# Window attention with global tokens: the order of a head's products on TensorE, and transposes of short key chunks

## The chip, the cores and the metric

The kernel runs on one core of one Trainium2 chip. The metric is the device time of one execution in microseconds, the median of the timed runs. Engine names in the rows: PE is TensorE's matrix product and PEld its weight load, DVE is VectorE, ACT is ScalarE, POOL is GpSimd, SP is the queue that issues most DMAs.

## The reference

There are 8 batches of 8 heads, 512 local tokens, 32 global tokens and a head width of 64. Global queries attend to all keys; local queries attend to the global keys and to a window of 32 positions on either side. The result goes through a feed-forward layer (width 512 to 2048 and back) with a squared ReLU, a scale and a bias.

```python
s_g = scale * q_g @ concat(k_g, k_l).T
out_g = sm(s_g) @ concat(v_g, v_l)
s_ll = where(abs(i - j) <= 32, scale * q_l @ k_l.T, -1e9)
a_l = sm(concat(scale * q_l @ k_g.T, s_ll))
out_l = a_l @ concat(v_g, v_l)
x = concat(out_g, out_l).transpose(0, 2, 1, 3).reshape(B * S, H * D)
h = x @ w_in
out = (s * relu(h) ** 2 + b) @ w_out
```

## The kernel before

A "half" is 256 local queries of one batch. There are 16 halves, and in each the 8 heads are worked one after the other; j counts them, 128 turns in all. The first 16 turns are worked as pairs of heads in plain float32; from turn 16 each head is worked alone, and its operands are split into a high and a low part so that the fast float32 format of TensorE can be used. A head's 256 queries are two blocks of 128; each block sees a strip of 192 or 224 keys, 416 in both blocks together (`COLS`). In the transposed probabilities each block has two chunks of keys: a whole one, 128 keys seen by all 128 queries, and a short one, of which only 64 or 96 keys and as many query columns are used (`CHUNKS`, whose entries are first key column, first query, number of queries).

Four kinds of products belong to a head on TensorE. The scores (line 363) are four: two blocks, each with the high and the low part of the queries as weights and the block's keys as moving columns (192 or 224). The global queries' product (line 376) has 64 weight columns and 256 or 288 moving ones. The transposes (line 316) are four, one for each chunk: the chunk of the probabilities is the weights and an identity matrix is what moves. The product with the values (line 407) is four, one for each chunk, with the values as 128 weight columns and 128, 192 or 256 moving ones.

The loop over j is a pipeline. In turn j TensorE computes the scores of head j, the transposes of head j-1 and the value products of head j-2, and then two pieces of the feed-forward, which lags by 10 turns: 24 products with 256 moving columns for piece m = j-10 (`ffn_in`, line 528) and 12 products with 512 for piece m-1 (`ffn_out`, line 561). Every eight turns there are also the transposes (line 455) and value products (line 478) of the global queries' rows. In PSUM there is one bank for the scores, one for the transposes (tag "t"), one for the value products and one for the global queries' products (tag "g"); the banks "t" and "g" are shared with the global rows' own transposes.

The order of TensorE's instructions is written out from turn 25 on (`ORDERED`, `manual_schedule`): from there the program's order is TensorE's order. Before turn 25, and on the other engines all along, a scheduler with a cost model places the instructions. Turn 25 itself issues its global queries' product late, behind the feed-forward piece.

In a turn of a first half the order on TensorE is: one score product, the global queries' product, three score products, two value products, three transposes, two value products, one transpose. In a second half the global queries' product stands behind the third score product. Before the transposes, `p_transposes` takes the two short chunks first. A transpose of a short chunk that begins at query 0 moves 96 columns of the identity, the others 128; all of them load 128 key columns as weights. Where a chunk needs fewer than 128 keys, the packed values have rows of zeros at the unused keys, and what stands there in the probabilities is multiplied by zero.

After a head's transposes, ScalarE (line 396) and VectorE (line 397) read the transposed probabilities out of PSUM and split them. After the global queries' product ScalarE (line 384) copies its low part and VectorE (line 385) adds the two.

Of the kernel before, what the change touches and what calls it, by code (L numbers as in the profile page):

```python
# [10 lines left out]
F32 = mybir.dt.float32  # L11
# [10 lines left out]
P = 128  # L22
# [10 lines left out]
CHUNKS = {  # L33
# [11 lines left out]
NF = 16  # L45
AHEAD = 0
LAG = 10
ORDERED = 25
# [19 lines left out]
def window_attention_then_ffn(ctx: ExitStack, tc: tile.TileContext, qd, qp, qg, kw, vw, vg, w_in, w_out, sv, bv, out):  # L68
# [23 lines left out]

    keep_busy(WARM_FIRST, "warm0")


# [200 lines left out]
    def chunks(j):  # L296
        b, hf, h = slot(j)
        o = 0
        for blk in range(2):
            for c in range(2):  # L300
                c0, q0, n = CHUNKS[hf, blk][c]
                yield blk, c, c0, q0, n, slice(o, o + n)
                o += n

# [3 lines left out]
    def p_transposes(j):  # L308
        sm = st_.pop(("p", j))
        p_t = ps.tile([P, 512], F32, tag="t", name=f"ps_t{j}")  # L310
        first = 64 if slot(j)[1] == 0 else 0
        st_["pst", j] = p_t[:, first:first + NC]
        for blk, c, c0, q0, n, o in sorted(chunks(j), key=lambda x: x[1]):
            at = first + o.start - q0
            q = 96 if c == 0 and q0 == 0 else P
            nc.tensor.transpose(out=p_t[:, at:at + q], in_=sm[0:q, c0:c0 + P], identity=ident[0:q, 0:q])  # L316
            yield
# [35 lines left out]
    def scores(j):  # L353
        b, hf, h = slot(j)
        ks, qs = st_.pop(("ks", j)), st_.pop(("qs", j))
        p_s = ps.tile([P, 512], F32, tag="s", name=f"ps_s{j}")
        late = j == ORDERED
        if not late:
            p_g = ps.tile([P, 512], F32, tag="g", name=f"ps_g{j}")
        for blk in range(2):  # L360
            cols = COLS[hf, blk]
            for a in range(2):
                nc.tensor.matmul(  # L363
                    p_s[:, cols], lhsT=qs[:, a, blk * P:(blk + 1) * P], rhs=ks[:, cols], start=(a == 0), stop=(a == 1),
                )
                if blk == hf and a == 0 and not late:
                    g_product(j, ks, p_g)
        softmax([j], [p_s])
        if late:
            st_["late", j] = ks  # L370
        else:
            g_sum(j, p_g)

# [12 lines left out]

    def late_scores(j):
        if ("late", j) in st_:
            p_g = ps.tile([P, 512], F32, tag="g", name=f"ps_g{j}")
            g_product(j, st_.pop(("late", j)), p_g)  # L390
            g_sum(j, p_g)
# [32 lines left out]

    def transposes_and_pv(jt, jp):
        t = p_transposes(jt) if NF <= jt < NS else iter(())
        p = pv_products(jp) if NF <= jp < NS else iter(())
        for which in (p, p, t, t, t, p, p, t):
            next(which, None)
        list(p), list(t)  # L430
        if NF <= jp < NS:
            pv_sum(jp)
        if NF <= jt < NS:
            p_split(jt)


# [11 lines left out]
    def g_transposes(b, g):  # L448
        sg = st_["sg", b, g]
        pg = st_["pg", b, g] = sb.tile([P, 5, 4, 2, SG], F32R, tag="pg", name=f"pg{b}_{g}", bufs=1)  # L450
        for c0, c1, tag in ((0, 4, "g"), (4, 5, "t")) if b else ((4, 5, "g"), (0, 4, "t")):
            p_t = ps.tile([P, 4, P], F32, tag=tag, name=f"ps_tg{b}_{g}_{c0}")
            for c in range(c0, c1):
                s0 = min(c * P, SGW - P)
                nc.tensor.transpose(out=p_t[:, c - c0, :], in_=sg[:, s0:s0 + P], identity=ident)
            v = p_t[:, 0:c1 - c0].rearrange("p c (h q) -> p (c h) q", h=4)
            ph, pl = (pg[:, c0:c1, :, i, :].rearrange("p c h q -> p (c h) q") for i in range(2))
            with tc.high_priority():
                nc.scalar.copy(out=ph, in_=v)
                nc.vector.tensor_sub(out=pl, in0=v, in1=f32(ph))  # L460
            yield
# [41 lines left out]
    def xg_split(t):  # L503
        xs = sb.tile([P, 8 * HALF + 56], F32R, tag="xs", name=f"xs{t}", bufs=1)
        xs = xs[:, 0:8 * HALF].rearrange("p (i c q) -> p i c q", i=2, c=4)
        for i in range(2):
            xr = sb.tile([P, 2 * NC], F32, tag="pt", name=f"xgr{i}")[:, 0:DM]
            nc.sync.dma_start(xr, xg_d[i * P:(i + 1) * P, :])
            p_t = ps.tile([P, 4, P], F32, tag="ts"[i], name=f"ps_xg{i}")
            for c in range(4):  # L510
                nc.tensor.transpose(out=p_t[:, c, :], in_=xr[:, c * P:(c + 1) * P], identity=ident)
            q = slice(i * P, (i + 1) * P)
            nc.scalar.copy(out=xs[:, 0, :, q], in_=p_t)
            nc.vector.tensor_sub(out=xs[:, 1, :, q], in0=p_t, in1=f32(xs[:, 0, :, q]))
        xs_[t] = xs
# [98 lines left out]
    for j in range(NM + LAG + 2):  # L614
# [18 lines left out]
        tr(j - 1)  # L633
        transposes_and_pv(j - 1, j - 2)
        vsp(j - 1)
# [7 lines left out]
        if 0 <= m < NM:  # L643
            ffn_in(m)
            late_scores(j)
            if m % 8 == 7:
# [88 lines left out]
```

## Time and profile before

| what | value |
|---|---|
| median of three runs | 1035.42 us (1033.2 to 1035.54) |
| the profiled execution, first to last instruction | 1034.0 us |
| its own time beside this span | the profile gives the span alone |
| TensorE products busy | 996.6 us, 96% of the span |
| TensorE weight loads busy | 903.5 us, 87% |
| VectorE, ScalarE, GpSimd busy | 805.9, 706.1, 300.9 us |
| mean granted TensorE clock | 0.982 of full speed |
| feed-forward products, lines 528 and 561, busy | 422.7 and 404.1 us |
| transposes, line 316, busy | 95.9 us in 512 in the page's group |
| value products, line 407; scores, line 363 | 90.7 and 77.5 us |

The two feed-forward groups make up 65% of the chain that ended last, the transposes 4%, the value products 4%, the scores 4%. Products overlap one another in the profile, since the next one starts while the last one drains: the duration of a single product is longer than the time by which it moves the end, and a sum of durations is not a time. The difference between the ends of two successive products is. Some records of products can be missing from a trace.

### The profile page before, as it was taken

How to read it: one execution, taken by the hardware profiler on the slowest of the kernel's cores; microseconds unless marked ns; L12 is line 12 of the kernel's file. 1: busy time of each engine (PE TensorE's matmuls, PEld its weight loads, DVE VectorE, ACT ScalarE, POOL GpSimd, SP SyncE). 2: the span in 40 equal slices, each digit the busy share in tenths (PEclk: the TensorE clock that was granted, in tenths of full speed). 3: DMA queues.
4: the chain of work that ended last, by engine and by line, in shares of the span. 5: the costliest groups of instructions: out<-in, count | busy, mean ns of one | idle time of the engine just before them, and what ended most of it. 6: DMA issues, size and time to landing. Idle time of an engine off the chain costs nothing.

```text
span 1034.0 us, 20232 instructions
## 1 busy us (share of the span) xinstructions
PE 996.6 (96%) x7060; PEld 903.5 (87%) x7060; DVE 805.9 (78%) x2036; ACT 706.1 (68%) x1786; POOL 300.9 (29%) x365
## 2 busy tenths in 40 slices
PE   5689999999999999999999999999999999999996
PEld 2368898899999999999999999999999999999995
DVE  6999778888878888888888888888888888873321
ACT  5986777677676777777677777777677777653221
POOL 0000444233433333333333432343323443211000
PEclk8869999999999999999999999999999999999999
DMA  8952222212321222213221222222221321101000
GB/s 326 344 177 68 88 81 84 76 59 86 91 70 57 71 88 76 74 55 97 78 79 53 70 90 71 79 63 91 73 78 58 95 72 45 42 24 35 12 21 21
DMA packets 62254, 85.73 MB, mean 83 GB/s; under 512 B 7368, under 2 KB 49352, under 8 KB 62152
## 3 DMA queue, kind: packets, MB, share of 16 engines
q1 hardware_dynamic: 61864, 83.39, 25.4%
q8 instruction: 56, 0.92, 0.4%
q10 hardware_dynamic: 288, 1.05, 0.3%
q14 instruction: 46, 0.38, 0.1%
HBM read 74.97 MB, written 9.44 MB: 82 GB/s over the span
## 4 chain that ended last, share of the span: by engine, by line
PE 80%; DVE 9%; ACT 4%; DMA 3%; issue 2%; POOL 0%; SPq 0%; ACTq 0%; DVEq 0%; POOLq 0%
PE ps_h L528 33%; PE acc L561 32%; PE ps_t L316 4%; PE ps_o L407 4%; PE ps_s L363 4%; DVE g L543 1%; PE ps_og L478 1%; PE ps_g L376 1%; DMA rq<-in_qd 1%; DVE x L420 1%; DVE r L535 1%; DVE sm L236 1%; DMA wst<-in_w_in 1%; ACT sm L227 1%; ACT kq L197 1%
## 5 line engine op out<-in xcount | busy, mean ns | idle before, releaser
L528 PE MATMUL ps_h<-xs,w 128*128 128x256 f32 x3264 | 422.7, 284 | 3.4 <-ACT xs L499 2.7
L528 PEld LDWEIGHTS ps_h<-xs,w 128*128 128x128 f32 x3264 | 399.8, 190 | 7.4 <-ACT xs L499 3.1
L561 PE MATMUL acc<-w,g 128*128 128x512 f32 x1632 | 404.1, 395 | 0.0
L561 PEld LDWEIGHTS acc<-w,g 128*128 128x128 f32 x1632 | 294.6, 188 | 57.6 <-ACT r L534 0.5
L543 DVE SCALAR_TENSOR_TENSOR g<-r,b_t,g 128x512 fp32r<-128x512 f32 x136 | 118.3, 870 | 56.1 <-ACT g L542 55.7
L534 ACT ACTIVATE r<-ps_h 128x512 f32<-128x512 f32 x136 | 81.2, 597 | 112.0 <-PE ps_h L528 105.7
L542 ACT ACTIVATE g<-r,b_t 128x512 fp32r<-128x512 f32 x136 | 98.4, 724 | 78.4 <-DVE r L535 77.7
L535 DVE SCALAR_TENSOR_TENSOR r<-ps_h,s_t,r 128x512 f32<-128x512 f32 x136 | 101.4, 746 | 64.3 <-ACT r L534 64.3
L200 POOL TENSOR_TENSOR kq<-rq,kq 128x256 fp32r<-128x256 f32 x112 | 85.2, 761 | 191.8 <-ACT kq L199 187.4
L198 POOL TENSOR_TENSOR kq<-rk,kq 64x416 fp32r<-64x416 f32 x56 | 61.3, 1095 | 257.7 <-ACT kq L197 249.5
L227 ACT ACTIVATE sm<-sm,nm 128x224 f32<-128x224 f32 (+1 forms) x256 | 119.7, 469 | 5.0 <-DVE nm L221 4.6
L208 POOL TENSOR_TENSOR vs<-rv,vs 128x256 fp32r<-128x256 f32 x112 | 91.6, 818 | 95.4 <-ACT vs L207 90.1
L316 PE MATMUL ps_t<-ident,sm 128*128 128x128 f32 (+1 forms) x512 | 95.9, 274 | 12.6 <-ACT ptp L323 8.2
L384 ACT COPY tg<-ps_g 32x256 f32<-32x256 f32 (+1 forms) x112 | 42.3, 378 | 72.1 <-PE ps_g L376 71.5
L407 PE MATMUL ps_o<-pt,vs 128*128 128x256 f32 x448 | 90.7, 284 | 0.0
L418 DVE TENSOR_TENSOR u<-ps_o,u 128x256 f32<-128x256 f32 x112 | 47.4, 423 | 45.0 <-ACT u L417 43.2
L221 DVE CUSTOM_DVE_ANT_0 sm<-ps_s,mask 128x192 f32<-128x192 f32 (+1 forms) x224 | 74.7, 371 | 9.7 <-PE ps_s L363 9.5
L470 POOL TENSOR_TENSOR vsg<-rvg,vsg 128x320 fp32r<-128x320 f32 x64 | 56.7, 906 | 79.3 <-ACT vsg L469 79.3
L363 PEld LDWEIGHTS ps_s<-kq 128*128 128x128 f32 x448 | 71.6, 189 | 7.1
L363 PE MATMUL ps_s<-kq 128*128 128x192 f32 (+1 forms) x448 | 77.5, 265 | 0.0
L316 PEld LDWEIGHTS ps_t<-ident,sm 128*128 128x128 f32 (+1 forms) x512 | 57.7, 143 | 17.3 <-ACT ptp L323 9.8
L407 PEld LDWEIGHTS ps_o<-pt,vs 128*128 128x128 f32 x448 | 67.8, 190 | 0.3
(76 smaller groups left out, 1211.3 us busy)
## 6 DMA issues: line engine op xcount, KB each, us to landing
rq<-in_qd SPq DMA_DIRECT2D x112, 128.0 KB, 2.3
rv<-in_vw SPq DMA_DIRECT2D x112, 128.0 KB, 2.0
rk<-in_kw SPq DMA_DIRECT2D x56, 208.0 KB, 2.4
rvg<-in_vg SPq DMA_DIRECT2D x32, 320.0 KB, 2.9
out<-o SPq DMA_DIRECT2D x34, 256.0 KB, 2.0
wst<-in_w_in SPq DMA_DIRECT2D x15, 512.0 KB, 6.1
wst<-in_w_out SPq DMA_DIRECT2D x15, 512.0 KB, 6.7
rvp<-in_vw SPq DMA_DIRECT2D x8, 256.0 KB, 4.7
```

The lines of the kernel that those rows point to most:

```text
L200: nc.gpsimd.tensor_sub(out=qs[:, 1, :], in0=rq, in1=f32(qs[:, 0, :]))
L208: nc.gpsimd.tensor_sub(out=vs[:, :, 1, :], in0=rv4, in1=f32(vs[:, :, 0, :]))
L227: nc.scalar.activation(out=p, in_=p, func=AF.Exp, bias=nm[:, n:n + 1], scale=-1.0, accum_out=ss[:, n:n + 1],)
L316: nc.tensor.transpose(out=p_t[:, at:at + q], in_=sm[0:q, c0:c0 + P], identity=ident[0:q, 0:q])
L363: nc.tensor.matmul(p_s[:, cols], lhsT=qs[:, a, blk * P:(blk + 1) * P], rhs=ks[:, cols], start=(a == 0), stop=(a == 1),)
L407: nc.tensor.matmul(p_o[:, blk, :, q0:q0 + n], lhsT=vs[:, 2 * blk + c], rhs=pt[:, :, o], start=(c == 1), stop=(c == 0),)
L528: nc.tensor.matmul(p_h[:, k], lhsT=wi[f][:, a, c, :], rhs=xs[:, e, c, :], start=(n == 0), stop=(n == 11),)
L534: nc.scalar.activation(out=r, in_=p_h, func=AF.Relu)
L535: nc.vector.scalar_tensor_tensor(out=r, in0=p_h, scalar=s_t, in1=r, op0=ALU.mult, op1=ALU.mult)
L542: nc.scalar.activation(out=g[:, 0], in_=r, func=AF.Identity, bias=b_t)
L543: nc.vector.scalar_tensor_tensor(out=g[:, 1], in0=r, scalar=b_t, in1=f32(g[:, 0]), op0=ALU.add, op1=ALU.subtract,)
L561: nc.tensor.matmul(oacc[t][i], lhsT=g[:, a, k, i * P:(i + 1) * P], rhs=wo[f][:, e, :], start=(pr == 0 and n == 0), stop=(pr == 7 and n == 5),)
```

## The change

The short chunks are transposed with only as many key columns as they use: 64 or 96 weight columns instead of 128, so that only 64 or 96 partitions of PSUM are written. The rest of the partitions must hold finite numbers, and so the bank of the transposes becomes one buffer for the whole kernel, `t_bank`, which VectorE sets to zero once. In the first half's first block the short chunk's 64 keys are now read from column 128, at the first partitions, and the packed values have their zero rows behind them instead of ahead. The short chunk of the second half's second block, 64 keys wide, now moves 128 identity columns where it moved 96; it stands last in the transposed columns, so that nothing overlaps it.

The order within a head changes: the whole chunk of the first block is transposed first, then the short chunks (96 keys, then 64), and the other whole chunk last. On TensorE a turn is now: four score products, three transposes, the global queries' product, two value products, one transpose, two value products. The readers of the global queries' product are issued at its new place too. Turn 25 still issues it late.

```diff
-    (0, 0): ((64, 64, 64), (0, 0, 128)),
+    (0, 0): ((128, 64, 64), (0, 0, 128)),
...
     keep_busy(WARM_FIRST, "warm0")
+    t_bank = ps.tile([P, 512], F32, tag="t", name="t_bank")
+    nc.vector.memset(t_bank, 0.0)
...
     def chunks(j):
         b, hf, h = slot(j)
         o = 0
-        for blk in range(2):
-            for c in range(2):
-                c0, q0, n = CHUNKS[hf, blk][c]
-                yield blk, c, c0, q0, n, slice(o, o + n)
-                o += n
+        for blk, c in ((0, 0), (0, 1), (1, hf), (1, 1 - hf)):
+            c0, q0, n = CHUNKS[hf, blk][c]
+            yield blk, c, c0, q0, n, slice(o, o + n)
+            o += n
...
     def p_transposes(j):
         sm = st_.pop(("p", j))
-        p_t = ps.tile([P, 512], F32, tag="t", name=f"ps_t{j}")
+        p_t = t_bank
         first = 64 if slot(j)[1] == 0 else 0
         st_["pst", j] = p_t[:, first:first + NC]
-        for blk, c, c0, q0, n, o in sorted(chunks(j), key=lambda x: x[1]):
+        whole, short = [], []
+        for chunk in chunks(j):
+            (whole if chunk[1] else short).append(chunk)
+        short.sort(key=lambda x: -x[4])
+        for blk, c, c0, q0, n, o in (whole[0], *short, whole[1]):
             at = first + o.start - q0
-            q = 96 if c == 0 and q0 == 0 else P
-            nc.tensor.transpose(out=p_t[:, at:at + q], in_=sm[0:q, c0:c0 + P], identity=ident[0:q, 0:q])
+            q = 96 if n == 96 else P
+            keys = P if c else n
+            nc.tensor.transpose(out=p_t[0:keys, at:at + q], in_=sm[0:q, c0:c0 + keys], identity=ident[0:q, 0:q])
             yield
...
     def scores(j):
...
-        late = j == ORDERED
-        if not late:
-            p_g = ps.tile([P, 512], F32, tag="g", name=f"ps_g{j}")
...
-                if blk == hf and a == 0 and not late:
-                    g_product(j, ks, p_g)
         softmax([j], [p_s])
-        if late:
-            st_["late", j] = ks
-        else:
-            g_sum(j, p_g)
+        st_["gk", j] = ks
...
-    def late_scores(j):
-        if ("late", j) in st_:
+    def g_scores(j):
+        if NF <= j < NS:
             p_g = ps.tile([P, 512], F32, tag="g", name=f"ps_g{j}")
-            g_product(j, st_.pop(("late", j)), p_g)
+            g_product(j, st_.pop(("gk", j)), p_g)
             g_sum(j, p_g)
...
-    def transposes_and_pv(jt, jp):
+    def transposes_and_pv(j, jt, jp):
         t = p_transposes(jt) if NF <= jt < NS else iter(())
         p = pv_products(jp) if NF <= jp < NS else iter(())
-        for which in (p, p, t, t, t, p, p, t):
-            next(which, None)
-        list(p), list(t)
+        for _ in range(3):
+            next(t, None)
+        g_late = j == ORDERED
+        if not g_late:
+            g_scores(j)
+        next(p, None), next(p, None)
+        list(t)
+        list(p)
         if NF <= jp < NS:
             pv_sum(jp)
         if NF <= jt < NS:
             p_split(jt)
+        return g_late
...
-            p_t = ps.tile([P, 4, P], F32, tag=tag, name=f"ps_tg{b}_{g}_{c0}")
+            if tag == "t":
+                p_t = t_bank.rearrange("p (c q) -> p c q", c=4)
+            else:
+                p_t = ps.tile([P, 4, P], F32, tag=tag, name=f"ps_tg{b}_{g}_{c0}")
...
-        transposes_and_pv(j - 1, j - 2)
+        g_late = transposes_and_pv(j, j - 1, j - 2)
...
             ffn_in(m)
-            late_scores(j)
+            if g_late:
+                g_scores(j)
...
-        _np.concatenate([z[:, :, 0:64], w[0][:, :, 128:192]], axis=2), w[0][:, :, 0:128],
+        _np.concatenate([w[0][:, :, 128:192], z[:, :, 0:64]], axis=2), w[0][:, :, 0:128],
```

## Rows read from the trace of the kernel before

On TensorE a row gives the weights' rows*columns and then the moving shape; a row with a count names the shape of its first product only.

**Rows 1.** By stretch: busy PE, PEld, DVE, ACT, POOL us, clock, DMA share, GB/s.
```profile
77.90:180.00 102.10, 102.10 (x747) 92.54 (x745) 82.65 (x199) 74.21 (x189) 33.07 (x37) 1.00 0.26 78
...
187.00:980.00 793.00, 791.74 (x5721) 732.56 (x5721) 638.45 (x1675) 551.01 (x1431) 259.75 (x308) 1.00 0.22 68
```

**Rows 2.** Timeline of TensorE, first-half head: start, us, line, output<-inputs, shape, count.
```profile
505.20 0.76 PE L478 MATMUL ps_og<-vsg,pg 128*64 128x128 f32 x10
505.80 2.97 PE L561 MATMUL acc<-w,g 128*128 128x512 f32 x12
508.61 0.25 PE L363 MATMUL ps_s<-kq 128*128 128x192 f32 x1
508.70 0.28 PE L376 MATMUL ps_g<-kq,qgs 128*64 128x256 f32 x1
508.81 0.49 PE L363 MATMUL ps_s<-kq 128*128 128x192 f32 x3
509.14 0.35 PE L407 MATMUL ps_o<-pt,vs 128*128 128x256 f32 x2
509.33 0.49 PE L316 MATMUL ps_t<-ident,sm 128*128 128x128 f32 x3
509.57 0.46 PE L407 MATMUL ps_o<-pt,vs 128*128 128x256 f32 x2
509.86 0.27 PE L316 MATMUL ps_t<-ident,sm 128*128 128x128 f32 x1
509.89 3.05 PE L528 MATMUL ps_h<-xs,w 128*128 128x256 f32 x24
512.78 2.90 PE L561 MATMUL acc<-w,g 128*128 128x512 f32 x12
```

**Rows 3.** Timeline of TensorE, second-half head.
```profile
536.30 0.47 PE L363 MATMUL ps_s<-kq 128*128 128x224 f32 x3
536.62 0.29 PE L376 MATMUL ps_g<-kq,qgs 128*64 128x288 f32 x1
536.75 0.25 PE L363 MATMUL ps_s<-kq 128*128 128x192 f32 x1
536.84 0.40 PE L407 MATMUL ps_o<-pt,vs 128*128 128x256 f32 x2
537.07 0.44 PE L316 MATMUL ps_t<-ident,sm 96*128 96x96 f32 x3
537.26 0.42 PE L407 MATMUL ps_o<-pt,vs 128*128 128x256 f32 x2
```

**Rows 4.** Timeline of TensorE in slices that hold one product of a kind.
```profile
509.33 0.29 PE L316 MATMUL ps_t<-ident,sm 128*128 128x128 f32 x1
...
536.84 0.30 PE L407 MATMUL ps_o<-pt,vs 128*128 128x256 f32 x1
```

**Rows 5.** Timeline of ScalarE and of VectorE, same first-half head.
```profile
509.01 0.37 ACT L384 COPY tg<-ps_g 32x256 f32<-32x256 f32 x1 [1.15 <-PE ps_g L376]
...
505.89 0.56 DVE L236 TENSOR_SCALAR sm<-sm,ss 128x192 f32<-128x192 f32 x2
```

**Rows 6.** VectorE's groups in the first 25 us: busy, mean ns, idle before.
```profile
L157 DVE TENSOR_SCALAR we<-wst 128x1024 int16<-128x1024 int16 x4 | 2.7, 686 | 7.0 <-DMA wst<-in_w_out 7.0
```

**Rows 7.** Timeline of TensorE where the global queries' product waits for its bank.
```profile
226.00 0.25 PE L363 MATMUL ps_s<-kq 128*128 128x192 f32 x1
...
226.30 0.30 PE L376 MATMUL ps_g<-kq,qgs 128*64 128x256 f32 x1
```

**Rows 8.** Line L376 in the long stretch: its engine idle before it.
```profile
  issue: 2.1, 6
```

**Rows 9.** Line L316 in the long stretch: its engine idle before it.
```profile
  DVE pg L460: 1.6, 6
```

**Rows 10.** TensorE's waits in the whole span: us, times, longest.
```profile
PE ps_g L376 <- DVE sg L385: 2.5, 1, 2.5
```

**Rows 11.** The chain that ended last: start, us, what, count.
```profile
183.88 4.36 PE ps_h L528 x24
```

More of the change, by code (lines that the diff above doesn't have):

```diff
@@ L508, in xg_split @@
             nc.sync.dma_start(xr, xg_d[i * P:(i + 1) * P, :])
-            p_t = ps.tile([P, 4, P], F32, tag="ts"[i], name=f"ps_xg{i}")
+            p_t = ps.tile([P, 4, P], F32, tag="s", name=f"ps_xg{i}") if i else t_bank.rearrange("p (c q) -> p c q", c=4)
             for c in range(4):
```

## The prediction

> **What bounds the kernel now.** I read the busy time by stretch first. From 77.9 to 180 us and from 187 to 980 us the matrix engine's array is busy 102.10 of 102.10 us and 791.74 of 793.00 us at the full clock, while VectorE has 638.45 and ScalarE 551.01 us of those 793 [rows 1]. So in nine tenths of the span the order and length of TensorE's own instructions set the time, and the other engines matter only where TensorE waits for them. I then took one head of each half apart on TensorE [rows 2, 3]. Products overlap in these rows, so I add start and duration to get each row's end; the difference of two successive ends is what a product really took. All durations below are such differences. The profile gives the profiled execution's span, 1034.0 us, and no other time for it; the three timed runs (1033.2 to 1035.54, median 1035.42) lie within 1.6 us of it. The sum is a difference made inside the 1034.0 us, and I put it on the median.
>
> **What a product costs.** The 24 feed-forward products end 2.81 us after the transpose ahead of them, 0.117 each for 256 moving columns; twelve of 512 columns take 2.74, 0.228 each [rows 2]. That is 0.44 ns a column and a few ns, so 128, 192, 224, 256, 288 columns take 0.060, 0.088, 0.102, 0.116, 0.130; the rows have 0.09 for 192 behind the global queries' product [rows 3]. Transposes stream slower: the last one of the first-half head takes 0.10, and 96, 96 and 128 columns together 0.27 [rows 2, 3]. I take 0.109 for 128 columns and 0.082 for 96.
>
> Some products take longer, each behind a short one. The next product's weights load while the present one streams, and what does not fit is exposed. A 256-column product behind a 192-column one ends 0.14 after it, 537.14 against 537.00 [rows 3, 4]: 0.025 over its own time, so a load of 128 weight columns takes 0.088 + 0.025 = 0.113. The other rows agree within their rounding: three score products take 0.32 instead of 0.292, by this figure 0.025 + 0.011 exposed; twelve 512-column products behind a 128-column one take 2.81 instead of 2.74, where 0.053 is due [rows 2]. The load of a transpose is shorter: 128 columns behind a 128-column product end 0.13 after it, 509.62 against 509.49 [rows 2, 4], some 0.019 over, which makes the load 0.079. A load of 64 columns (the global queries' product behind a 192-column one, 0.12) exposes nothing [rows 2].
>
> **The new order, first half of a block of heads.** Before: S192 G S192 S224 S224 P256 P128 T128 T96 T128 P256 P192 T128, then the feed-forward (S scores, G the global queries' product, P values, T transposes). Exposed: 0.025 + 0.011 + 0.011 + 0.019, and 0.004 twice for a 0.113 load behind a transpose of 0.109: 0.074. After: S192 S192 S224 S224 T128 T96 T128 G P256 P128 T128 P256 P192. Exposed: 0.025 twice, because G no longer covers a score load; 0.011; nothing for the first T behind S224; 0.019; 0.004; and 0.025 for the feed-forward's first load behind P192, where a transpose stood: 0.109. That is +0.035 a head.
>
> **Second half.** Before: S224 S224 S192 G S192 P256 P192 T96 T96 T128 P256 P128 T128: 0.011 + 0.011 + 0.025 + 0.019 + twice 0.004 = 0.074. After: S224 S224 S192 S192 T128 T96 T128 G P256 P192 T128 P256 P128: 0.011 + 0.011 + 0.025 + 0.004 and 0.053 for the feed-forward's load behind the 128-column P: 0.104, so +0.030. Also, the 64-key chunk is now transposed over 128 query columns where it had 96: 0.109 instead of 0.082, +0.027.
>
> With TensorE's order as written from head 26 on, there are 48 score turns of the first half and 54 of the second: 48 x 0.035 + 54 x 0.030 = 3.3 us, and with the wider transpose in 55 heads 1.5 us: +4.8.
>
> **The shorter loads.** They save nothing here by these rows: a 96-key load stands behind a transpose of 0.109 and a 64-key load behind one of 0.082, and the old load of 0.079 was already shorter than both. Bounds: 0, and 0.019 a head if a short load stood where the exposed one is, which it does not (the exposed one is the whole chunk behind P128). I take 0.
>
> What the transpose itself costs with 64 or 96 key columns stands in no row. At most it is unchanged, since its moving columns set it in the rows (96 against 128). At least it falls in proportion: 0.109 to 0.055 and 0.082 to 0.061. G with 64 weight columns takes 0.12 for 256 moving columns, as much as the feed-forward with 128 [rows 2]; I take no change, nearest to that row.
>
> For this the Trainium skill, "TensorE: Matmul & The Clock Gate", section "LDWEIGHTS (loading the stationary operand)", has the rule that a load costs its columns divided by 1.2 ns, whatever the contraction: 107, 80 and 53 ns, as estimates from that page, for 128, 96 and 64. For the other products' 128 columns the rows agree (0.113); for the transposes they do not (0.079). By the rule the short loads would pay; that is the second rival.
>
> **Waits that move.** Transposes reach TensorE earlier: 0.44 us after the scores begin instead of 0.72 (G, P256 and P128 no longer ahead). Their usual inputs are ready: the softmax's last step ends at 506.45 for transposes at 509.33 [rows 2, 5], so 2.6 us of cover is left. Not so where the one-chunk evacuation of the global probabilities ends last: six waits, 1.6 us in all [rows 9], each 0.28 longer: +1.7. Conversely G arrives 0.65 later. It waits six times for its bank in the long stretch [rows 8]; the one shown ends 0.35 after the product ahead of it, 0.23 too late [rows 7]; with 0.65 of delay these waits go: 1.4 in all at that size and 2.1 by the row's total, of which I take -1.6. G's two readers (a ScalarE copy, a VectorE add) move with it. ScalarE's copy already waits 1.15 us for G [rows 5] with the next head's key split queued behind it; 0.65 more per head is inside ScalarE's idle third [rows 1], so 0; a head is 6.98 us [rows 2], so ScalarE's idle is about 2.1 us of it, and beyond that each 0.1 us of wait would cost 0.1 us a head. The products P end about 0.1 us later, and their readers have that slack.
>
> At 180 us G waits 2.5 us for VectorE's add of the head before [rows 10]; one score product and three transposes, 0.4 us, now stand ahead of it in addition: -0.4. Behind this idle time the clock falls to its lower level, and 24 feed-forward products take 4.36 instead of 2.81 [rows 2, 11]. Whether 2.1 us of idle still does that I cannot read; I leave it as it is.
>
> The bank set to zero once costs one VectorE instruction; VectorE idles 7.0 us for the first weights [rows 6], so 0 (uncovered, 0.3 to 0.7, since that row's 1024-element step takes 0.69). The fixed bank has the same two readers to wait for; no DMA moves. In the first 180 us, where the order is planned by a scheduler's costs, eight paired heads get the wider transpose and ten single heads the new order: +0.5 by the same prices, but the plan itself can shift by some 3 us either way.
>
> Sum: 4.8 + 1.7 - 1.6 - 0.4 + 0.5 = +5.0, so 1040 us.
>
> **Rivals.**
> 1. Not slower: a transpose streams by its key columns. Then every head gains 0.055 + 0.021 on two transposes, 103 heads x 0.076 = 7.8 us, and +5.0 becomes -2.8: 1032.6. It decides from a gain of 0.05 us a head on. For: no row shows a transpose with fewer keys. Against: G above, and 96 against 128 moving columns at equal keys.
> 2. Short loads pay. If transposes loaded like the others (0.113 for 128, 0.085 and 0.056 for the short), the old order would expose 0.110 in first-half heads and 0.141 in second-half ones, the new 0.064 and 0.050. Instead of +4.8 the array part is then about -1.3 (48 x -0.011 and 54 x -0.015): 1034. Against: the three second-half transposes would take 0.36, and take 0.27 [rows 3].
> 3. The 2.5 us wait at 180 us vanishes, because VectorE's add is planned elsewhere, and with it the low clock: -2.1 and -1.5 more, 1036.4. For: the readers of G are re-planned. Against: they hang on the same instruction.
> 4. The early plan or the moved readers go wrong by 3 to 4 us: 1043.5.
>
> **Chances.** Forecast 0.60 (own range 1037.5 to 1042.5), rival 1 0.10, rival 2 0.06, rival 3 0.14, rival 4 0.10. About 0.3%, 3.1 us, is what a measurement of this kernel can tell from no change, so slower begins at 1038.5: 0.53 of the forecast's chance and all of rival 4's, 0.63; faster is less than half of rivals 1 and a little of 2 and 3, 0.08; the same 0.29. The range leaves out rival 1 below and the far end of rival 4 above: 1034 to 1044.
>
> **What would show it.** On TensorE, end to end: the second and third score products 0.11 each in a first-half head; the feed-forward's first product about 0.14 and 0.17 behind the last P; a 64-key transpose 0.11 (rival 1: under 0.09); loads of the short chunks shorter in their rows without a shorter transpose group (rival 2: the group shrinks). The long stretch's waits of G gone and those of the transposes near 0.5 us each. The prediction would be wrong if the 6.98 us head [rows 2] did not grow by some 0.04 to 0.06, or if head 26's scores, now at 180 us, began more than 3 us earlier or later.

## The result: slower by 0.9%, and the profile after

The changed kernel takes 1044.43 us (1043.94 to 1045.13, four runs) where the kernel before takes 1035.38 beside it: a ratio of 1.0092, with a 95% interval of 1.0078 to 1.0106. The forecast was 1040.0 and the range ended at 1044, so the direction was right and the time 4.4 us too low, 0.4 above the range. The profiled execution's span is 1043.2 us against 1034.0, +9.2; head 26 begins its scores at 179.66 us in it (179.65 before), so the whole difference lies behind that point.

By stretch (columns as in [rows 1]), TensorE is still never idle in the early stretch, but in the long one 8.6 us of 793 are, where 1.3 were:

```profile
78.00:180.00 102.00, 102.00 (x747) 92.64 (x745) 85.85 (x203) 74.13 (x191) 32.17 (x38) 1.00 0.27 82
187.00:980.00 793.00, 784.40 (x5634) 725.68 (x5633) 628.28 (x1666) 547.38 (x1425) 260.48 (x308) 1.00 0.23 68
```

TensorE's timeline for a first-half head (it answers to [rows 2]), up to the scores of the second-half head behind it:

```profile
507.76 2.99 PE L568 MATMUL acc<-w,g 128*128 128x512 f32 x12
510.59 0.60 PE L366 MATMUL ps_s<-kq 128*128 128x192 f32 x4
511.04 0.47 PE L322 MATMUL t_bank<-ident,sm 128*128 128x128 f32 x3
511.26 0.36 PE L374 MATMUL ps_g<-kq,qgs 128*64 128x256 f32 x1
511.46 0.34 PE L405 MATMUL ps_o<-pt,vs 128*128 128x256 f32 x2
511.64 0.29 PE L322 MATMUL t_bank<-ident,sm 128*128 128x128 f32 x1
511.68 0.45 PE L405 MATMUL ps_o<-pt,vs 128*128 128x256 f32 x2
511.97 2.99 PE L535 MATMUL ps_h<-xs,w 128*128 128x256 f32 x24
514.80 2.93 PE L568 MATMUL acc<-w,g 128*128 128x512 f32 x12
517.57 0.59 PE L366 MATMUL ps_s<-kq 128*128 128x224 f32 x4
```

The new order is there. End to end, the three transposes (128, 96 and 128 moving columns) take 511.51 - 511.19 = 0.32, no less than moving columns alone would give. A head, from the end of one group of 512-column products to the end of the next (510.75 to 517.73), takes 6.98. Over all heads without global-row work the median of that is 6.97 in first halves and 6.98 in second halves, where it was 6.92 and 6.93: +0.05 each, where the forecast's sums had 0.035 and 0.057. (The forecast wrote 6.98 for the head of before; by [rows 2] it is 515.68 - 508.77 = 6.91. No term of the sum hung on it, only the 2.1 us of ScalarE's idle time and the first sign of being wrong.)

The rest stands in the list of TensorE's waits (us, times, longest), in the line that answers to [rows 9]; the 2.5 us of [rows 10] is not in the list any more:

```profile
PE t_bank L322 <- DVE pg L467: 7.8, 7, 1.3
```

Taken apart by ends, from head 26 on: the products' own times with their exposed loads grew by 4.8 us. Six first transposes after a global-row evacuation come 1.47 us late and six more 0.35, 11.4 with one at the end, where before six came 0.32 late, 1.9: +9.5. The six waits of the global queries' product are gone: -1.6. The wait at 180 us fell from 2.7 to 0.2, -2.5, and with it went the low clock, -1.5. That makes +8.7 of the 9.2; some 0.5 is spread over small intervals.

### The profile page after: what moved, and what is told of

It is laid out like the page before. It is cut to its first block, busy times and chain, and to the rows that moved or that the text cites. A ratio compares the mean times of both kernels' runs of the same rounds, so it can differ in the third digit from the quotient of the medians.

```text
span 1043.2 us, 20121 instructions
## 1 busy us (share of the span) xinstructions
PE 1001.7 (96%) x7060; PEld 907.5 (87%) x7060; DVE 802.0 (77%) x2037; ACT 705.7 (68%) x1786; POOL 300.6 (29%) x365
## 4 chain that ended last, share of the span: by engine, by line
PE 86%; DVE 6%; ACT 4%; DMA 3%; issue 1%; SPq 0%; ACTq 0%
PE ps_h L535 35%; PE acc L568 33%; PE t_bank L322 5%; PE ps_s L366 4%; PE ps_o L405 4%; PE ps_og L485 2%; PE ps_g L374 1%; DMA wst<-in_w_out 1%; DMA rqp<-in_qp 1%; DMA wst<-in_w_in 1%; ACT sm L229 1%; DVE x L418 1%; DVE r L542 1%; PE ps_op L337 1%; DVE pg L467 1%
## 5 line engine op out<-in xcount | busy, mean ns | idle before, releaser
L535 PE MATMUL ps_h<-xs,w 128*128 128x256 f32 x3264 | 416.2, 282 | 3.5 <-ACT xs L506 2.9
L535 PEld LDWEIGHTS ps_h<-xs,w 128*128 128x128 f32 x3264 | 396.9, 189 | 7.3 <-ACT xs L506 3.3
L542 DVE SCALAR_TENSOR_TENSOR r<-ps_h,s_t,r 128x512 f32<-128x512 f32 x136 | 101.1, 744 | 59.8 <-ACT r L541 59.7
L550 DVE SCALAR_TENSOR_TENSOR g<-r,b_t,g 128x512 fp32r<-128x512 f32 x136 | 103.7, 762 | 54.0 <-ACT g L549 52.6
L541 ACT ACTIVATE r<-ps_h 128x512 f32<-128x512 f32 x136 | 81.5, 599 | 68.7 <-PE ps_h L535 64.7
L210 POOL TENSOR_TENSOR vs<-rv,vs 128x256 fp32r<-128x256 f32 x112 | 86.7, 774 | 108.8 <-ACT vs L209 102.3
L322 PE MATMUL t_bank<-ident,sm 128*128 128x128 f32 (+2 forms) x512 | 97.2, 276 | 19.6 <-ACT ptp L329 8.3
L395 DVE TENSOR_TENSOR pt<-t_bank,pt 128x416 fp32r<-128x416 f32 x112 | 66.1, 590 | 44.6 <-ACT pt L394 43.6
L238 DVE TENSOR_SCALAR sm<-sm,ss 128x192 f32<-128x192 f32 (+1 forms) x224 | 77.6, 388 | 3.4
L322 PEld LDWEIGHTS t_bank<-ident,sm 128*128 128x128 f32 (+2 forms) x512 | 56.6, 132 | 26.4 <-DVE pg L467 11.2
L405 PE MATMUL ps_o<-pt,vs 128*128 128x256 f32 x448 | 75.4, 281 | 0.0
L366 PEld LDWEIGHTS ps_s<-kq 128*128 128x128 f32 x448 | 67.2, 190 | 9.1
L418 DVE TENSOR_TENSOR x<-u 64x256 f32<-64x256 f32 x112 | 71.9, 642 | 3.6
```

The costliest lines, as they stand in the source:

```text
L210: nc.gpsimd.tensor_sub(out=vs[:, :, 1, :], in0=rv4, in1=f32(vs[:, :, 0, :]))
L322: nc.tensor.transpose(out=p_t[0:keys, at:at + q], in_=sm[0:q, c0:c0 + keys], identity=ident[0:q, 0:q])
L366: nc.tensor.matmul(p_s[:, cols], lhsT=qs[:, a, blk * P:(blk + 1) * P], rhs=ks[:, cols], start=(a == 0), stop=(a == 1),)
L405: nc.tensor.matmul(p_o[:, blk, :, q0:q0 + n], lhsT=vs[:, 2 * blk + c], rhs=pt[:, :, o], start=(c == 1), stop=(c == 0),)
L418: nc.vector.tensor_add(out=x[q0:q0 + 64, h // 2, :].rearrange("p (k q) -> p k q", k=2), in0=u[0:64], in1=u[64:128],)
L535: nc.tensor.matmul(p_h[:, k], lhsT=wi[f][:, a, c, :], rhs=xs[:, e, c, :], start=(n == 0), stop=(n == 11),)
```

## Where the late transposes come from

VectorE's, ScalarE's and TensorE's timeline around one of the six, in the kernel after:

```profile
248.22 1.10 PE L535 MATMUL ps_h<-xs,w 128*128 128x256 f32 x8
...
249.91 0.42 DVE L416 TENSOR_TENSOR u<-ps_o,u 128x256 f32<-128x256 f32 x1
250.07 0.61 ACT L541 ACTIVATE r<-ps_h 128x512 f32<-128x512 f32 x1
...
250.44 0.85 DVE L418 TENSOR_TENSOR x<-u 64x256 f32<-64x256 f32 x1
...
251.32 0.56 DVE L238 TENSOR_SCALAR sm<-sm,ss 128x192 f32<-128x192 f32 x2
251.80 0.74 DVE L542 SCALAR_TENSOR_TENSOR r<-ps_h,s_t,r 128x512 f32<-128x512 f32 x1
...
252.46 0.68 DVE L467 TENSOR_TENSOR pg<-ps_tg,pg 128x512 fp32r<-128x512 f32 x1
...
254.00 0.28 DVE L467 TENSOR_TENSOR pg<-t_bank,pg 128x128 fp32r<-128x128 f32 x1
...
254.34 0.52 PE L322 MATMUL t_bank<-ident,sm 128*128 128x128 f32 x3 [1.25 <-DVE pg L467]
```

and the same turn in the kernel before:

```profile
250.72 1.94 PE L528 MATMUL ps_h<-xs,w 128*128 128x256 f32 x15
...
252.74 0.60 ACT L534 ACTIVATE r<-ps_h 128x512 f32<-128x512 f32 x1
...
254.25 0.74 DVE L535 SCALAR_TENSOR_TENSOR r<-ps_h,s_t,r 128x512 f32<-128x512 f32 x1
...
256.45 0.28 DVE L460 TENSOR_TENSOR pg<-ps_tg,pg 128x128 fp32r<-128x128 f32 x1
...
256.79 0.52 PE L316 MATMUL ps_t<-ident,sm 128*128 128x128 f32 x3
```

The transposes wait for the bank, which still holds one chunk of global probabilities; the last to read it is VectorE's 128-column step (L467, before L460). Count from the end of the 24 feed-forward products (249.32 and 252.66). The evacuation ends 4.96 later in the kernel after and 4.07 before: VectorE is 0.89 late, and it is so already at its step `r` (L542, before L535), which starts 2.48 behind the products where it started 1.59. The relu (L541, before L534) is late too, 0.75 against 0.08, but `r` does not wait for it: the relu ended at 250.68, `r` starts at 251.80, and VectorE has been at work without a gap since 249.91. In the long stretch VectorE stands waiting for the relu in 9 of 110 turns, and did in 11 of 112. So the lateness comes down VectorE's own row of work.

It is there one turn earlier. The products, the relu, VectorE's last two softmax steps and its `r`, and GpSimd's split in that turn, after:

```profile
238.69 2.99 PE L535 MATMUL ps_h<-xs,w 128*128 128x256 f32 x24
...
241.72 0.60 ACT L541 ACTIVATE r<-ps_h 128x512 f32<-128x512 f32 x1
...
242.89 1.26 DVE L238 TENSOR_SCALAR sm<-sm,ss 128x192 f32<-128x192 f32 x2
243.15 1.74 POOL L477 TENSOR_TENSOR vsg<-rvg,vsg 128x320 fp32r<-128x320 f32 x2 [1.05 <-ACT vsg L476]
244.08 0.74 DVE L542 SCALAR_TENSOR_TENSOR r<-ps_h,s_t,r 128x512 f32<-128x512 f32 x1
```

and before, where GpSimd's split starts at 246.51, behind `r`:

```profile
242.31 2.74 PE L528 MATMUL ps_h<-xs,w 128*128 128x256 f32 x22
...
245.08 0.60 ACT L534 ACTIVATE r<-ps_h 128x512 f32<-128x512 f32 x1 [0.57 <-PE ps_h L528]
...
245.22 0.57 DVE L236 TENSOR_SCALAR sm<-sm,ss 128x192 f32<-128x192 f32 x2
...
245.72 0.75 DVE L535 SCALAR_TENSOR_TENSOR r<-ps_h,s_t,r 128x512 f32<-128x512 f32 x1
```

The relu starts 0.04 behind its products (241.68 and 245.05) in both, yet `r` starts 2.40 behind them where it started 0.67, in all six turns alike. 0.69 of this is the pair of softmax steps, which now runs beside GpSimd's split.

Behind it stands ScalarE, whose results VectorE's softmax, splits and sums read. Measured from a turn's first score, ScalarE's copy of the global queries' product starts at 0.64 us in the median turn of before and at 1.07 after, the key split behind it at 0.94 and at 1.63. In the median turn VectorE's `r` then starts 1.54 behind the products where it started 0.97, while the relu starts 0.04 behind them in both. In the six late turns themselves the copy does not wait for the product (which ends at 1.03, the copy starts at 2.1): ScalarE is still behind from the turn before. What the experiments can show is whether the product's place sets this off; the way from ScalarE to VectorE's queue is read from these rows and is argued.

## Experiments

Theory A: the later place of the global queries' product delays ScalarE's queue and through it the evacuation. Rival B: the values at the end of the head do it (their readers come later). Rival C: it is the transposes' own earlier place. Then what removed the waits of before: the order, the bank, the short loads, or the early plan. In every one of these kernels the scheduler also places the instructions of VectorE, ScalarE and GpSimd anew, so a part of the change is always tested together with the plan that comes of it. Ratios are to the kernel before on the same chip, with 95% intervals.

**Rows early** (after, with the transposes of the global rows all ahead of the 512-column products).

```diff
-            next(turn, None)
+            if i == 0:
+                list(turn)
```


> The changed kernel, with both of the global rows' transpose groups ahead of the first six 512-column products of the turn instead of one ahead of each six. Everything else is as in the changed kernel. Both theories say that the changed kernel loses most of its time where the transposes wait for the evacuation of the global rows' one-chunk group (six waits of 1.47 us, six of 0.35, 0.5 at the end: 11.4 us). Here that group is evacuated some 1.4 us earlier: waits of at most 2 us in all, 1035 to 1037 us. Rival: the time went into the products themselves or into VectorE as a whole; then no less than 1042 us.


1038.3 us, 1.0033 (1.0020 to 1.0047). A little above what both theories said. The late transposes shrink to six of about 0.36 and six of about 0.26; the second global-row group now waits 0.28 for the bank six times. So 6 us of the loss hang on when that chunk is evacuated.

**Values first** (after, with two value products ahead of the three transposes, and the global queries' product still behind these).

```diff
+        next(p, None), next(p, None)
         for _ in range(3):
             next(t, None)
...
-        next(p, None), next(p, None)
-        list(t)
         list(p)
+        list(t)
```


> The changed kernel with the value products back ahead of the transposes (scores, two value products, three transposes, global product, two value products, one transpose). Theory A: the evacuation is late because the global product now comes 0.65 us later and ScalarE's copy of it stands at the head of ScalarE's queue, so the feed-forward's steps and the evacuation behind them are late. Then the waits stay, each shorter only by the 0.19 us by which the transposes come later: 1041 to 1042 us. Theory B: it is late because the value products are last, and their sums on ScalarE and VectorE stand ahead of the feed-forward's. Then the evacuation is back at 0.9 us behind the first score product and the waits at 0.3 to 0.4 us: 1035.5 to 1037 us.


1061.04 us, 1.0254 (1.0238 to 1.0269). Both missed the size. 28.7 us of waits stand in it; the relu starts over 2.3 us late in one turn of ten, and the copy of the global queries' product at about 2.2 in the median turn. Moving the values forward, which B held to be the cure, made it much worse: B falls. That it is so bad because the product comes later still is not shown: it ends at 1.25 in the median turn, and the copy starts 0.8 behind it, so ScalarE is late by more than the product.

**Short chunks only** (the order of before with the short loads, the fixed bank and the wide 64-key transpose).

```diff
-        for _ in range(3):
-            next(t, None)
...
+        for which in (p, p, t, t, t, p, p, t):
+            next(which, None)
...
+                if blk == hf and a == 0 and j != ORDERED:
+                    g_product(j, ks, p_g)
```


> The products in the order of before (global product among the scores, values, short chunks first), with the short loads, the fixed bank and the 128-column transpose of the 64-key chunk. By the prices of the products: +1.5 us for the wider transpose, -0.9 because a 64-key load now stands behind the 128-column value product in the first half, waits as in the kernel before: 1035.4 to 1037 us. Rival: the short transposes or the fixed bank cost something by themselves: 1039 us and more.


1031.04 us, 0.9962 (0.9949 to 0.9975): faster than both kernels, and the best here. The array costs +0.6 as priced, but the wait at 180 us and the six of the global queries' product are gone as well, which neither expectation had.

**Global product back** (after, with that product among the scores as before; the transposes stay ahead of the values).

```diff
-        if not g_late:
-            g_scores(j)
...
+                if blk == hf and a == 0 and j != ORDERED:
+                    g_product(j, ks, p_g)
```


> The changed kernel with the global product back among the scores; transposes still ahead of the values. Theory A: the evacuation of the one-chunk group is back at about 0.9 us behind the first score product, the transposes' waits at 0.4 to 0.5 us, the global product's waits of before (0.24 us, and perhaps the 2.7 us one at 180 us with the low clock) come back: 1036 to 1039.5 us. Theory B: the waits stay at 1.3 to 1.4 us and the global product's come on top: 1041 to 1045 us.


1034.62 us, 0.9995 (0.9985 to 1.0004), below A's range and far from B's. Six late transposes are left, 0.52 by ends:

```profile
PE t_bank L322 <- DVE pg L471: 1.8, 6, 0.3
```

This one move is 9.8 us, 2.2 of them in the array. ScalarE's key split starts at 0.94 in the median turn, as before, and in the turns ahead of the late ones VectorE's pair takes 0.57 and `r` starts 0.86 behind the products (2.39 in the kernel after). So the product's later place sets the long waits off. C's share is what the forecast had for the transposes' earlier place, six of 0.5.

**Copy on VectorE** (after; VectorE instead of ScalarE copies that product's low part).

```diff
-nc.scalar.copy(out=tg[0:32, 0:ng], in_=p_g[32:64, 0:ng])
+nc.vector.tensor_copy(out=tg[0:32, 0:ng], in_=p_g[32:64, 0:ng])
```


> The changed kernel with the ScalarE copy of the global product moved to VectorE, the products' order unchanged. Theory A1: the late global product delays ScalarE because its copy stands at the head of ScalarE's queue. Then ScalarE goes on at once, the evacuation comes back by some 0.7 us and the transposes' waits fall from 1.47 to 0.7 us or less: 1037 to 1040 us. Theory A2: ScalarE waits because the global product is now the last reader of its head's keys, and the next split into that key buffer, which follows the copy in the queue, waits for it as well. Then the wait only passes to the split, and VectorE has 0.3 us more a head: 1044 us or more.


1038.32 us, 1.0027 (1.0017 to 1.0037), with the product itself as late as in the kernel after. The transposes' waits:

```profile
PE t_bank L322 <- DVE pg L467: 1.5, 6, 0.3
```

A1 has the time, but ScalarE does not go on at once: its key split, now at the head of the row, stands waiting for the product, as A2 said (us, times, in the long stretch):

```profile
  PE ps_g L374: 94.0, 79
```

What is gone from ScalarE is the copy's 0.39 us. The key split starts at 1.07 in the median turn (1.63 in the kernel after), and `r` in the turns ahead of the six at 0.88 behind the products. With the product as late as before and 0.4 us more a head on VectorE, the time falls by 6.1 us: it is ScalarE's row that must not come late, and neither ScalarE's waiting by itself nor VectorE's load.

**Global product right behind the scores** (after; 0.1 to 0.35 us later than in the kernel before and 0.3 earlier than in the kernel after).

```diff
+        if not g_late:
+            g_scores(j)
         for _ in range(3):
             next(t, None)
-        if not g_late:
-            g_scores(j)
```


> The changed kernel with the global product straight behind the four score products, ahead of the three transposes: 0.30 us earlier than in the changed kernel, 0.35 later than with it among the scores. A dose between the two (transposes' waits 1.47 and 0.52 us). Theory A, the global product's place passes its delay on in full: waits of 0.8 to 1.1 us in the six turns, 1036.5 to 1039 us; if only the very last place is harmful, 0.5 us and 1035 us.


1036.3 us, 1.0010 (1.0001 to 1.0019).

```profile
PE t_bank L322 <- DVE pg L467: 1.7, 6, 0.3
```

The copy starts at 0.76 in the median turn and the key split at 1.16; `r` in the turns ahead of the late ones starts 1.10 behind the products. "Passes its delay on in full" is false: the first 0.1 us of the copy's delay costs the transposes no wait more than with the product back among the scores, the next 0.3 cost 8 us of them. Where between the two the cost begins is not shown.

**Fixed bank only** (before, with the one zeroed bank).

> The kernel before, with nothing but the transposes' bank made one fixed buffer, set to zero once. The products, their order and their shapes are those of before. All kernels with the change's parts so far lost the 2.5 us wait at 180 us and the low clock behind it, and the global product's waits with it. If the fixed bank does that: 1030.5 to 1032.5 us, and none of these waits. If it is a matter of where VectorE stands when GpSimd's work runs beside it, and the short loads or the order shifted that: 1035 us, waits as before.


1035.14 us, 0.9996 (0.9987 to 1.0006), every wait as before. The bank is free, and it is not what removed the waits.

**Long loads** (short chunks only, with 128 key columns loaded again).

```diff
-            keys = P if c else n
+            keys = P
```


> The kernel with the order of before, short loads and fixed bank (1031.0 us), in which all four transposes load 128 key columns again; the chunks' places, the fixed bank and the wider transpose of the 64-key chunk stay. By the prices the transpose behind the 128-column value product shows 0.019 us again in 48 heads: +0.9, 1032 us. If the short loads were what took the 2.5 us wait at 180 us and the global product's waits away, these come back: 1036 us.


1044.38 us, 1.0090 (1.0076 to 1.0105), and not for the reason tested. Behind head 26 it costs 0.45 us. But head 26 begins at 192.0 us instead of 179.1: what lies ahead of it, where the scheduler places most of the work, came out 12.9 us longer. 7.4 of these lie in the turn of head 25, where a wait for VectorE's add like the one at 180 us stands one turn earlier, with slow products behind it (granted clock 0.50 from 185.5 to 188.3 us):

```profile
182.35 0.50 PE L376 MATMUL ps_g<-kq,qgs 128*64 128x288 f32 x1 [3.25 <-DVE sg L385]
...
184.58 4.77 PE L533 MATMUL ps_h<-xs,w 128*128 128x256 f32 x24
```

The six later waits of the global queries' product stay away. So the short loads are not what took those; for the wait at 180 us this kernel decides nothing, since its early plan is another.

**Narrow short chunks** (short chunks only, moving just the 64 or 96 query columns that are used, which for the first half come from 64 partitions).

```diff
-            q = 96 if n == 96 else P
+            q = slice(q0, q0 + n)
```


> The kernel with the order of before, short loads and fixed bank, in which a short chunk is also transposed with only the 64 or 96 query columns that it uses (64 moving identity columns instead of 128, from 64 partitions). The price of the moving columns says 0.109 to 0.057 us for the 64-key chunk, 0.052 x 103 heads: 5.4 us off 1031.0, that is 1025 to 1026.5 us. If a transpose has a floor near 0.08 us, 1028 us; if 64 partitions cost a change of the array's setting, 1031 us or more.


1055.03 us, 1.0192 (1.0177 to 1.0207). A transpose with 64 rows takes 0.17 end to end, three times what its columns would, and the one behind it 0.13 to 0.15 more. The group of three, with fewer columns, ends 0.50 after the product ahead of it (513.24 against 512.74), where it ended 0.33 in [rows 2]:

```profile
512.39 0.35 PE L409 MATMUL ps_o<-pt,vs 128*128 128x256 f32 x2
512.67 0.57 PE L318 MATMUL t_bank<-ident,sm 64*64 64x64 f32 x3
```

Against the kernel with the short chunks only, 19 us of the profiled execution lie behind head 26 and 7 ahead of it, where the plan is another.

**The 64-key transpose at 96 columns** (short chunks only, the second half's 64-key chunk moving 96 columns as before).

```diff
-            q = 96 if n == 96 else P
+            q = 96 if q0 == 0 and not c else P
```


> The kernel with the order of before, short loads and fixed bank (1031.0 us), in which the 64-key chunk of the second half moves 96 query columns again instead of 128, as the kernel before did. By the price of moving columns 0.109 becomes 0.082 in 55 heads: -1.5 us, 1029.5 us. If a 64-key transpose of 96 rows costs a change of setting, as one of 64 rows did, 12 us more.


1034.61 us, 0.9999 (0.9990 to 1.0008). The array saves its 1.5 us, but the waits of before are all back, 2.9 at 180 us and six of 0.22 to 0.44, and the low clock with them. So 27 ns on one transpose of every second-half head decide some 5 us.

**Width alone** (the kernel before, with that transpose at 128 columns and nothing else).

```diff
-            q = 96 if c == 0 and q0 == 0 else P
+            q = 96 if c == 0 and q0 == 0 and n == 96 else P
```


> The kernel before with one edit: the 64-key chunk of the second half moves 128 identity columns in its transpose where it moved 96; order, loads, bank and key columns as before. It asks which part of the change rids the order written out of its waits for VectorE at 180 us (2.7 us and the low clock behind it) and six times later (0.24 us each). Theory W (the width of this transpose is what re-plans VectorE and ScalarE): these waits go, -2.5 -1.5 -1.5, the transposes cost +1.5: 1031 to 1032.5. Rival V (the plan hangs on the kernel as a whole, no part by itself decides): the waits stay as in before and the price alone is seen, 1036.5 to 1037.5; or the plan of the first 180 us moves otherwise, by several us either way, which is seen in the time at which turn 26 begins.


1031.73 us, 0.9968 (0.9956 to 0.9980): faster for a step that costs 1.5 us by itself. Theory W holds for this kernel. VectorE and GpSimd ahead of head 26, kernel before:

```profile
177.20 0.86 DVE L230 TENSOR_SCALAR ss<-ss 128x2 f32<-128x2 f32 x1
...
178.12 0.74 POOL L200 TENSOR_TENSOR kq<-rq,kq 128x256 fp32r<-128x256 f32 x1
178.30 1.39 DVE L236 TENSOR_SCALAR sm<-sm,ss 128x224 f32<-128x224 f32 x2
178.82 0.76 POOL L208 TENSOR_TENSOR vs<-rv,vs 128x256 fp32r<-128x256 f32 x1
...
182.12 0.45 DVE L385 TENSOR_TENSOR sg<-ps_g,tg 32x288 f32<-32x288 f32 x1
```

and with the width alone:

```profile
175.67 0.73 POOL L200 TENSOR_TENSOR kq<-rq,kq 128x256 fp32r<-128x256 f32 x1
...
176.16 0.26 DVE L230 TENSOR_SCALAR ss<-ss 128x2 f32<-128x2 f32 x1
...
177.48 0.55 DVE L236 TENSOR_SCALAR sm<-sm,ss 128x224 f32<-128x224 f32 x2
...
180.00 0.45 DVE L385 TENSOR_TENSOR sg<-ps_g,tg 32x288 f32<-32x288 f32 x1
```

The scheduler placed the early work anew, GpSimd's splits come earlier and overlap VectorE's softmax steps by no more than some 0.2 us each, these take 0.3 to 0.4 of the time, and the add for which TensorE waits at 180 us comes 2.1 us sooner.

**After at 96 columns** (the same edit in the kernel after).

> The kernel after with one edit: the 64-key chunk of the second half moves 96 identity columns again where it moves 128. By its columns it should save 1.5 us in TensorE's array. Theory W (in these kernels the width of this one transpose places VectorE's and ScalarE's early work, whatever the order of the products): the wait at 180 us is back, 2 to 3 us of idle and the low clock behind it, and the time is 1043.5 to 1047 in spite of the saving. Theory G (in the kernel after it is the later place of the global queries' product that has made this wait go): the wait stays at 0.2 us and the time falls by the saving alone, to 1042 to 1043.3. The six long waits of the transposes should stay at 1.47 us in both.


1041.94 us, 1.0063 (1.0046 to 1.0080). The wait at 180 us stays small (0.4), as theory G said, and the time falls by the array's 1.5 and the six smaller waits of the transposes. In the order of the change that wait is gone without the width; whether the later product or the plan as a whole does it is not separated. The six long waits stay at 1.47.

In sequence, then: 1035.4 before; the width 1031.7; the short loads and the bank 1031.0; the transposes ahead of the values 1034.6; the global queries' product behind them 1044.4. (The second step, 0.7, is too small to tell from none.)

## Why the prediction was right or wrong

- **The array, +4.8: right**, 4.82 measured. The prices of loads hold in the new places. A 64-key transpose takes 0.112 end to end behind a 96-column one, as a 128-key one does there in the kernel before: the key columns don't matter, the moving ones do, and rival 1 falls. With short loads the transposes of the new order take no less than those with long ones took; rival 2 falls. By the Trainium skill, "TensorE: Matmul & The Clock Gate", section "LDWEIGHTS (loading the stationary operand)", a load's time goes with its columns. The short loads agree with it only where a load is exposed: in the old order the transpose behind the 128-column value product takes 0.127 with a 128-key load and 0.109 with a 64-key one, the 0.019 a head that the prediction gave as the upper bound.
- **The step that failed: "0.65 more per head is inside ScalarE's idle third [rows 1], so 0".** The price was taken from idle time summed over a turn. But idle time behind the row of work that the copy heads is no cover for that row: everything in it comes later, and VectorE reads it. ScalarE's key split started 0.69 later in the median turn, VectorE's `r` 0.57 later, and 1.7 later in the turn ahead of each long wait; so the evacuation came 0.89 late. Putting the product back took 9.8 us off, taking its copy from ScalarE 6.1. The prediction's own point, "beyond that each 0.1 us of wait would cost 0.1 us a head", was put at 2.1 us of idle time. The cost set in well below: a copy 0.43 later in the median turn cost 8 us of waits, one 0.12 later none.
- **The transposes' waits, +1.7: wrong by that step**, +9.5. With the product in its old place these waits are 0.52 each, near the forecast's 0.28 + 0.28; the other 0.95 in each of six, and six new ones of 0.35, come with the product's later place.
- **The waits of the global queries' product, -1.6: right.**
- **The wait at 180 us, -0.4: wrong**, -2.5 and -1.5 more for the clock. That is rival 3, whose price (-3.6 more) holds and whose chance was 0.14. Without this gain the time would have been about 1048: that the forecast missed by only 4.4 us is luck.
- **The early part, +0.5: right within its bounds** (0.0), though the runs show that its bounds were far too narrow: of 3 us either way, one run used 12.9.
- **The set of the bank, 0: right**, shown by the kernel with the fixed bank alone.
- **Rival 4** gave 1043.5, nearest to the result, by "the moved readers". The mechanism was named and not worked out.

Left open: which instruction of the early plan moves first when one transpose gets wider; how much of VectorE's lateness is waiting for ScalarE and how much its steps beside GpSimd's; and what the later product would cost with the other engines' order held as it was.

## What to carry to other kernels

An engine's idle share is no cover for an instruction that heads a row of its work: ask who reads the rest of that row, and follow the delay through those engines to the step that TensorE waits for. Before moving a product, ask who reads it: with the same late product, its copy on VectorE instead of ScalarE was worth 6.1 us. Where a scheduler places part of a kernel, an edit of 27 ns can change the time by several us either way, so each part of a change is to be timed by itself.

## What the runs showed of the hardware

- A 64-row transpose among 128-row transposes and products took 0.173 us where its columns would give 0.057, and the transpose behind it 0.13 to 0.15 more (narrow short chunks).
- VectorE's steps stretch beside GpSimd's: the pair L236 takes 1.39 us beside two splits and 0.55 nearly alone. By the Trainium skill, "SBUF — State Buffer", section "SBUF: two separate sides", VectorE and GpSimd share a pair of ports that one instruction holds for its whole length while the other waits; for VectorE that is so when its instruction is in a two-port mode or has two inputs in SBUF. The rows fit it: the pair's 0.84 more is somewhat over one split (0.74). No run here shows which of VectorE's steps take the shared pair.
- At 180 us the 24 products behind 2.5 us of idle took 4.36 us [rows 11]; the granted clock was 0.50 in this stretch, the lower of the clock's two levels. In the kernel after they follow almost without a gap, end 2.88 us after the value product ahead of them (184.29 against 181.41), and the granted clock is 1.00. TensorE there, and the stretches of before and after (columns as in [rows 1]):

```profile
180.98 0.43 PE L405 MATMUL ps_o<-pt,vs 128*128 128x256 f32 x2
181.25 3.04 PE L535 MATMUL ps_h<-xs,w 128*128 128x256 f32 x24
```

```profile
183.80:186.60 2.80, 2.80 (x15) 2.80 (x15) 2.70 (x9) 2.55 (x9) 2.44 (x3) 0.50 0.16 34
```

```profile
181.40:184.20 2.80, 2.80 (x26) 2.80 (x25) 2.68 (x9) 2.75 (x9) 2.10 (x2) 1.00 0.17 47
```
